# A planned attention kernel: wide QK matmuls dropped where the plan has TensorE columns to spare, and softmax tiles and shifts placed anew

## The chip, the cores and the metric

The kernel runs on one core of one Trainium2 chip. The metric is the device time of one execution in microseconds (us), lower is better. Each number called a median is over several executions; a profile is one further look at one execution, with its span from the first to the last instruction (about 2 us less than the time). All runs quoted here are in the fast state. A ratio is the mean time of one kernel's fast runs over the mean of the other's in the same rounds on the same chip, so it is not quite the ratio of the medians beside it. In the profile PE is TensorE, ACT ScalarE, DVE VectorE, POOL GpSimd, SP the queue that issues most DMAs.

## The reference

```python
B, H, S, Dh = 1, 32, 2048, 20            # all inputs bfloat16
def reference(q, k, v, t):
    eps = 1e-6
    qn = q / (jnp.sqrt((q * q).sum(axis=-1, keepdims=True)) + eps)
    kn = k / (jnp.sqrt((k * k).sum(axis=-1, keepdims=True)) + eps)
    logits = jnp.einsum('bhqd,bhkd->bhqk', qn, kn) * t[None, :, None, None]
    attn = softmax(logits, axis=-1)
    return jnp.einsum('bhqk,bhkd->bhqd', attn, v)
```

There are 32 x 2048 x 2048 exponentials and a head size of only 20, so the exponentials, not the matmuls, are the bulk of the work.

## The kernel before

The work of a head is cut into 16 tiles (128 keys by 2048 queries, four units of 512). Most tiles go through ScalarE, which reads logits in PSUM and writes exponentials. The others go through VectorE, which makes the exponential out of integer arithmetic: one evacuation of PSUM per half tile into int16 (read as fp16), then three shifted copies of the tile. GpSimd takes part of the third shifts. One table says how many tiles of each head VectorE has, another for how many of these GpSimd makes the third shift.

```python
    DVE_TILES = [4, 4, 4, 5, 5, 5, 5, 5, 4, 5, 5, 5, 5, 5, 4, 5, ...]      # sum 153
    KDN = (3, 3, 3, 3, 3, 3, 3, 3, 3, 3, 3, 3, 3, 3, 3, 2, ...)
    # evacuation, two per tile:            DVE
    e.tensor_scalar(xt[sx][:, o:o + W1], psD[:, slot * W1:slot * W1 + W1], X_MUL, X_ADD, ALU.mult, ALU.add)
    # shifts, three per tile of 128 x 2048: DVE, the third one on POOL in pieces of 128 x 512 int32 where KDN says so
    e.tensor_scalar(dst[:, 0:w], x, float(PHASES[i]), None, ALU.add)
```

A QK matmul contracts over 20 values, padded to 32 rows. TensorE runs matmuls of different row groups side by side, so a ScalarE wave of three units (a wave is what one exponential instruction takes) can take one matmul slot (in the trace three such matmuls start within 10 ns, and two of 128 rows 0.22 to 0.23 us apart). Each wave also has a wide form: it feeds 64 or 128 rows, the extra ones zero, which no longer fit beside one another and take one slot more. The wide form computes the same. It exists only to keep TensorE's load up, because a lightly loaded array loses its clock (experiment 3 shows it).

```python
    if len(us) == 3: qk.modes = [("q3", 32, PE_MM + 0.01, 384.0), ("q2", 64, PE_MM * 2, 768.0)]   # rows, us, columns of load
    else:            qk.modes = [("q2", 64, PE_MM, 256.0 * len(us)), ("qk", 128, PE_MM * len(us), 512.0 * len(us))]
```

The whole program is ordered before it runs: a list scheduler with a cost for each task fixes one static order per engine, and the engines then wait for one another by semaphores. The planner repeats this; in each pass it looks at every window of 3.41 us, and where the load of finished matmuls is under 3500 it makes some QK groups wide. It never takes one back.

```python
        heavy = set()
        for _ in range(self.PASSES):
            for t in choice:
                tag, t.rows, t.dur, t.work = t.modes[t in heavy]
            self.list_schedule()
            ...                                   # windows of TICK = 3.41 us, floor LOAD = 3500
                    while i and load < self.LOAD and m >= i:
                        ...
                            more.add(u)
            if not more: break
            heavy |= more
```

## Time and profile before

The median is 667.6 us (666.9 to 668.7, 4 runs).

| | busy us | share | what it does |
|---|---|---|---|
| ACT | 657.1 | 99% | 287 exponentials of 128x1536, 287 of 128x1024, one rest |
| DVE | 654.2 | 98% | 306 evacuations, 365 shifts, small work |
| PE | 601.3 | 90% | QK and PV matmuls; ends are modelled, so this share is too high |
| POOL | 355.3 | 53% | 188 half shifts, norms, scaling |

The page of the kernel before: busy time and clock over the span, the chain that ended last, and the costliest groups (line, engine, operation, output and input, count, busy us, mean ns, idle before).

```profile
span 665.3 us, 14541 instructions
...
PE 601.3 (90%) x5914; PEld 166.3 (25%) x5959; DVE 654.2 (98%) x927; ACT 657.1 (99%) x584; POOL 355.3 (53%) x364
...
PEclk9999999999999999999999999999999999999999
...
ACT 90%; DVE 5%; DMA 1%; SPq 1%; PE 1%; POOL 0%; issue 0%; ACTq 0%
...
L757 ACT ACTIVATE p_ring<-psA 128x1024 bf16<-128x1024 f32 (+1 forms) x575 | 650.0, 1371 | 2.8 <-PE psA L666 2.7
L803 DVE TENSOR_SCALAR xt<-psD 128x1024 int16<-128x1024 f32 x306 | 371.1, 1213 | 4.4 <-PE psD L666 3.3
L821 POOL TENSOR_TENSOR ss<-xt,two 128x512 int32<-128x512 int32 x188 | 236.0, 1256 | 163.2 <-DVE ss L815 83.4
...
L815 DVE TENSOR_SCALAR ss<-xt 128x2048 int16<-128x2048 int16 x365 | 241.8, 683 | 0.9
...
```

ScalarE is busy from its first exponential to its last, and the chain is its exponentials for 89% of the span. VectorE is as full. A reader might stop here and say that nothing can be gained except by moving work. But the records of one engine overlap (the groups' mean of 1371 ns times 575 is 788 us, not 650), so a short wait need not show as idle time. The safer reading is from one start to the next in the timeline: at the median a 128x1536 exponential takes 1.330 us and a 128x1024 one 0.904 us. The sum of what lies above these medians I call the excess. It is 11.0 us for ScalarE, of which the waits view shows 2.7 us:

The waits of ScalarE in the kernel before (who waited for whom: us in total, times, longest).

```profile
...
ACT p_ring L757 <- PE psA L666: 2.7, 4, 1.3
...
```

Of the 11.0 us, 3.8 us are four stalls of over 0.4 us (1.57, 1.20, 0.55 and 0.45 us, behind the exponentials that start at 28.6, 52.6, 209.6 and 221.3 us); the other 7.2 us are small slips. In front of the first three stalls TensorE, whose order is fixed, stood waiting for a DMA or for VectorE (timeline of the kernel before; the wait is in brackets):

```profile
...
30.64 0.37 PE L666 MATMUL psA<-qz,kR 32*128 32x512 bf16 x1 [1.47 <-DMA qz<-qkT]
...
53.93 0.38 PE L666 MATMUL psD<-qz,kR 128*128 128x512 bf16 x1 [0.96 <-DVE xt L803]
...
210.25 0.39 PE L666 MATMUL psD<-qz,kR 64*128 64x512 bf16 x1 [0.73 <-DVE xt L803]
...
```

How much is wide can be counted from the weight loads of QK with 128 rows (groups by shape, kernel before; the count stands after the x):

```profile
...
L666 PEld LDWEIGHTS psA<-qz,kR 128*128 128x128 bf16 x129 | 8.7, 97 | 26.1 <-ACT p_ring L757 24.3 <-issue 1.4
...
L666 PEld LDWEIGHTS psD<-qz,kR 128*128 128x128 bf16 x58 | 4.4, 97 | 7.8 <-DVE xt L803 5.8 <-DVE rec L702 0.5 <-issue 0.5
...
L666 PEld LDWEIGHTS psA<-qz,qkT 128*128 128x128 bf16 x36 | 3.2, 97 | 6.5 <-ACT p_ring L757 5.8 <-issue 0.5
...
L666 PEld LDWEIGHTS psD<-qz,qkT 128*128 128x128 bf16 x20 | 1.8, 96 | 5.2 <-DVE xt L803 3.9 <-issue 1.1
...
```

That is 243 loads. With the three-unit waves of 64 rows it makes the 180 wide groups that the planner reports.

### The profile page before, as it was taken

The numbers are of one execution on the slowest core, as the hardware profiler recorded it, in microseconds if no ns is written. First come the engines' busy times: TensorE is split into PE (matmuls) and PEld (weight loads), VectorE is DVE, ScalarE is ACT, GpSimd is POOL, SyncE is SP. The second block draws the span as 40 slices with busy tenths as digits, with TensorE's granted clock in tenths as the row PEclk, the third lists the DMA queues.
The fourth block names the chain that finished last, engine by engine and source line by source line (L and its number), as shares of the span: only waits on it lengthen the run. The fifth ranks groups of instructions, "written<-read, shape, count | busy, mean of one in ns | idle before, by whom it ended". The sixth has DMA issues, their size and how long they took to land.

```text
span 665.3 us, 14541 instructions
## 1 busy us (share of the span) xinstructions
PE 601.3 (90%) x5914; PEld 166.3 (25%) x5959; DVE 654.2 (98%) x927; ACT 657.1 (99%) x584; POOL 355.3 (53%) x364
## 2 busy tenths in 40 slices
PE   7798989989889999898999999999899989999987
PEld 2222222222222222222222222222222222222221
DVE  8999999999999999999999999999999999999997
ACT  9999999999999999999999999999999999999997
POOL 2346664573655645565365446556466566655622
PEclk9999999999999999999999999999999999999999
DMA  5554434134242442544035142352414415231200
GB/s 64 67 80 76 65 48 78 19 78 54 41 81 21 81 51 45 89 62 75 4 74 62 32 79 28 68 68 44 80 17 91 45 30 81 39 80 11 55 6 11
DMA packets 196723, 36.24 MB, mean 54 GB/s; under 512 B 172592, under 2 KB 196656, under 8 KB 196656
## 3 DMA queue, kind: packets, MB, share of 16 engines
q1 hardware_dynamic: 196512, 35.22, 34.5%
q8 instruction: 47, 0.77, 0.5%
q14 instruction: 20, 0.16, 0.1%
q10 hardware_dynamic: 144, 0.08, 0.1%
HBM read 7.87 MB, written 2.62 MB: 16 GB/s over the span
## 4 chain that ended last, share of the span: by engine, by line
ACT 90%; DVE 5%; DMA 1%; SPq 1%; PE 1%; POOL 0%; issue 0%; ACTq 0%
ACT p_ring L757 89%; DVE xt L803 3%; DVE ss L815 2%; SPq L404 1%; DMA qk_sb<-in_q_dram 1%; DMA qkT<-qkn 0%; ACT qz L450 0%; PE psA L666 0%; PE psD L666 0%; DMA qz<-qkT 0%; POOL qkn L561 0%; POOL ss L821 0%; DVE oT L699 0%; ACT L440 0%; PE psO L686 0%
## 5 line engine op out<-in xcount | busy, mean ns | idle before, releaser
L757 ACT ACTIVATE p_ring<-psA 128x1024 bf16<-128x1024 f32 (+1 forms) x575 | 650.0, 1371 | 2.8 <-PE psA L666 2.7
L803 DVE TENSOR_SCALAR xt<-psD 128x1024 int16<-128x1024 f32 x306 | 371.1, 1213 | 4.4 <-PE psD L666 3.3
L821 POOL TENSOR_TENSOR ss<-xt,two 128x512 int32<-128x512 int32 x188 | 236.0, 1256 | 163.2 <-DVE ss L815 83.4
L666 PE MATMUL psA<-qz,kR 32*128 32x512 bf16 (+2 forms) x1051 | 227.2, 384 | 36.4 <-ACT p_ring L757 27.7
L815 DVE TENSOR_SCALAR ss<-xt 128x2048 int16<-128x2048 int16 x365 | 241.8, 683 | 0.9
L686 PE MATMUL psO<-ss,vph 128*32 128x512 f16 x1836 | 172.9, 385 | 0.1
L686 PE MATMUL psO<-p_ring,vaug 128*32 128x512 bf16 x1436 | 132.9, 384 | 0.1
L666 PE MATMUL psA<-qz,qkT 32*128 32x512 bf16 (+2 forms) x354 | 117.6, 384 | 12.6 <-ACT p_ring L757 10.3
L666 PE MATMUL psD<-qz,kR 64*128 64x512 bf16 (+1 forms) x454 | 120.9, 384 | 7.9 <-DVE xt L803 4.8
L666 PEld LDWEIGHTS psA<-qz,kR 32*128 32x128 bf16 (+2 forms) x1077 | 54.4, 92 | 181.0 <-ACT p_ring L757 176.2
L494 POOL TENSOR_SCALAR vph<-vaug 128x160 f16<-128x160 bf16 (+1 forms) x96 | 40.0, 417 | 80.8 <-DMA vaug<-in_v_dram 39.8
L561 POOL TENSOR_TENSOR qkn<-qk_sb,rs_r 128x640 bf16<-128x640 bf16 x29 | 47.5, 1639 | 37.4 <-DVE ss L815 19.0
L686 PEld LDWEIGHTS psO<-ss,vph 128*32 128x32 f16 x1836 | 44.3, 94 | 81.4 <-issue 56.5
L686 PE MATMUL psO<-xt,vaug 128*32 128x512 f16 x612 | 60.3, 385 | 0.0
L666 PE MATMUL psD<-qz,qkT 64*128 64x512 bf16 (+1 forms) x144 | 54.3, 385 | 1.4 <-DVE xt L803 0.9
L686 PEld LDWEIGHTS psO<-p_ring,vaug 128*32 128x32 bf16 x1436 | 35.7, 94 | 52.4 <-issue 44.1
L666 PEld LDWEIGHTS psD<-qz,kR 64*128 64x128 bf16 (+1 forms) x459 | 29.6, 93 | 68.3 <-DVE xt L803 50.8
L666 PEld LDWEIGHTS psA<-qz,qkT 64*128 64x128 bf16 (+2 forms) x359 | 28.5, 92 | 58.4 <-ACT p_ring L757 55.1
L710 POOL TENSOR_TENSOR o_stage<-oT,rec 128x320 bf16<-128x320 f32 x30 | 29.0, 967 | 18.3 <-DVE ss L815 14.3
L528 DVE TENSOR_REDUCE rs_sum<-sq 128x32 f32<-128x640 bf16 x32 | 25.7, 806 | 0.1
L699 DVE STREAM_TRANSPOSE oT<-psO 128x512 f32<-128x512 f32 x32 | 22.5, 704 | 1.0 <-PE psO L686 1.0
L686 PEld LDWEIGHTS psO<-xt,vaug 128*32 128x32 bf16 x612 | 15.8, 94 | 28.1 <-issue 20.8
(46 smaller groups left out, 87.3 us busy)
## 6 DMA issues: line engine op xcount, KB each, us to landing
kR<-qkT SPq DMA_DIRECT2D x62, 96.0 KB, 2.2
qz<-qkT SPq DMA_DIRECT2D x124, 32.0 KB, 1.8
kR<-qkT SPq DMA_DIRECT2D x62, 64.0 KB, 2.0
qk_sb<-in_k_dram SPq DMA_DIRECT2D x32, 80.0 KB, 2.6
vaug<-in_v_dram SPq DMA_DIRECT2D x32, 80.0 KB, 3.7
qk_sb<-in_q_dram SPq DMA_DIRECT2D x124, 20.0 KB, 2.6
out_dram<-o_stage SPq DMA_DIRECT2D x31, 80.0 KB, 2.2
kR<-qkT SPq DMA_DIRECT2D x62, 32.0 KB, 1.9
```

The source lines that it names most:

```text
L404: return add(eng, name, lambda e, tk: e.dma_start(dst, src), dur, deps, pri, lat=lat, dma=key)
L494: vsc[h] = [add("POOL", f"vs{h}", lambda e, tk, i=i: e.tensor_scalar(vph[bv][:, i, 0:nd, :], vaug[bv][:, R - nd:R, :], 2.0 ** (-PHASES[i] ...
L528: sums.append(dv("sum", lambda e, tk, i=i, sqb=sqb: e.tensor_reduce(rs["sum"][:, 2 * R * i:2 * R * (i + 1)], sqb[:, :, :], AXIS_X, ALU.add ...
L561: u = add("POOL", f"norm{h}", lambda e, tk, x=x, b=b, i=i, j=j: e.tensor_tensor(qkn[b][:, j:j + m, 0:D], x[:, j:j + m, :], bc(rs["r"][:, 2 ...
L666: return eng.matmul(dst, lhsT, mov, tile_position=(p0, 0))
L686: last = eng.matmul(psO[32 * g:32 * g + 32, :], w, rhs_of(g), start=start, stop=False, skip_group_check=True, tile_position=(0, 32 * g))
L699: trO[h] = add("DVE", f"tr{h}", lambda e, tk: e.transpose(oT[:, :, :].rearrange("p r d -> p (r d)"), psO[:, :]), 0.63, [lambda: pv_users[h ...
L710: fin[h] = add("POOL" if pool else "DVE", f"fin{h}", lambda e, tk: e.tensor_tensor(st, src, rb, ALU.mult), TTDUR if pool else 0.40, [rc] + ...
L757: act[w] = add("ACT", f"exp{w}", lambda e, tk: e.activation(p_ring[:, p0 * 512:p0 * 512 + n], psA[:, slot * WAVES[0] * 512:slot * WAVES[0] ...
L803: t1_prev[nchunk[0]] = add("DVE", f"t1.{j}.{k}", lambda e, tk, o=o, slot=slot: e.tensor_scalar(xt[sx][:, o:o + W1], psD[:, slot * W1:slot ...
L815: sh.append([dv(f"s{i}.", lambda e, tk, i=i, dst=dst: e.tensor_scalar(dst[:, 0:w], x, float(PHASES[i]), None, ALU.add), 0.533, war)])
L821: u = add("POOL", f"s{i}.{js[0]}.{c}", lambda e, tk, i=i, dst=dst, c=c, n=n: e.tensor_tensor(dst[:, 2 * c:2 * (c + n)].bitcast(I32), xt[sx ...
```

## The change

The intent: the planner may now also take a wide matmul back where the load of every window that it counts in stays 300 above the floor, so that TensorE has fewer slots to serve and ScalarE and VectorE wait less. Constants of the scheduler and both tables are placed anew for that plan; VectorE gets 154 tiles instead of 153, GpSimd 99 third shifts instead of 94. The diff, cut to its core:

```diff
-    SWITCH = 0.25
+    SWITCH = 0.5
-    PASSES = 10
+    PASSES = 12
+    FIRM = 4
+    MARGIN = 300.0
-    DSL = 0.8
-    HOLDA = 9.0
+    DSL = 0.6
+    HOLDA = 0.7
-    HOLD = {"DVE": 0.0, "PE": HPE}
+    HDV = 0.08
+    HOLD = {"DVE": HDV, "PE": HPE}
...
+            drop, more = set(), set()
+            if k < self.PASSES - self.FIRM:
+                for m, u in enumerate(pe):
+                    if u in heavy and u.modes[1][2] > u.modes[0][2] + 0.02 and \
+                            min(loads[m:hi[m] + 1]) - gain(u) >= self.LOAD + self.MARGIN:
+                        drop.add(u)
...
-            heavy |= more
+            heavy = heavy - drop | more
...
-    SPREAD = 1.0
+    SPREAD = 0.8
-    DVE_TILES = [4, 4, 4, 5, 5, 5, 5, 5, 4, 5, 5, 5, 5, 5, 4, 5, 5, 5, 5, 5, 4, 5, 5, 5, 5, 5, 4, 5, 5, 5, 5, 5]
+    DVE_TILES = [4, 4, 4, 5, 5, 5, 5, 5, 4, 5, 5, 5, 5, 4, 5, 5, 5, 5, 5, 5, 4, 5, 5, 5, 5, 6, 5, 5, 5, 4, 4, 6]
-    KDN = (3, 3, 3, 3, 3, 3, 3, 3, 3, 3, 3, 3, 3, 3, 3, 2, 3, 3, 3, 3, 3, 3, 3, 3, 3, 4, 3, 3, 3, 4, 2, 3)
+    KDN = (4, 5, 2, 4, 3, 2, 4, 4, 2, 2, 4, 3, 3, 3, 4, 2, 4, 3, 3, 4, 3, 3, 5, 2, 3, 5, 2, 4, 2, 3, 3, 2)
+    ACCN = (0, 0, 0, ...)                     # tiles whose third shift a DMA would make: none
...
+        cst = sbuf("cst", [128, 2048], I16)
+        z_cst = memset("POOL", cst[:, :], PHASES[2], 0.3, -70)
```

Left out of this cut are a further step in the choice of what is made wide, a later moment at which GpSimd is asked for its next task, and another choice of which tiles of a head GpSimd helps with. The last two lines belong to a path in which a DMA would add the shift. Its table is all zeros.

## The prediction

> **What bounds the kernel now.** ScalarE and VectorE together. Busy (part 1 of the page): ACT 657.1 us (99%), DVE 654.2 (98%) of 665.3; PE 601.3 (90%, inflated by pipelining), POOL 355.3. The chain of waits is ACT exponentials for 88.8%, unbroken from 222.7 to 660.6 us. Start to start in the timeline, the 128x1536 exponential costs 1.330 us and the 128x1024 one 0.904 (medians); 287 pairs make 641 us, against 652.7 from the first (8.4) to the end of the last (661.1). So ACT loses about 11 us to late matmuls: two stalls of 1.6 and 1.2 us before 55 us, 1 us near 210 to 222, the rest in some 40 slips of 0.05 to 0.3 us that the waits view hides (it shows 2.7 us), because records overlap. DVE is alike: last shift ends 660.6, start-to-start excess about 14 us, half of it dependences of startup and tail. Granted clock 1.00 up to 640 us.
>
> **What the change does.**
> 1. One more head tile goes from ACT to DVE (153 to 154). ACT saves 4/5 of a pair, 1.8 us. DVE gains two evacuations (2 x 1.13 us).
> 2. POOL takes 99 instead of 94 of the third shifts; DVE shifts go from 365 to 363, -1.2 us. DVE net +1.1 us. POOL gains 10 halves of 1.26 us, in windows of DVE's PSUM reads.
> 3. Wide QK matmuls. By weight loads, about 83 two-unit and 58 three-unit ACT groups and 42 DVE groups are wide, some 180; each costs one more matmul slot (about 0.22 us). They only keep TensorE's column load up. The plan may now drop those with over 300 columns to spare; I guess a third to a half go: 13 to 20 us of TensorE time, little of it critical. What counts is the share of ACT's 8 us and DVE's 7 us of slips that such slots caused: I guess a third.
> 4. Ordering constants: small, unknown sign.
>
> The DMA-accumulate path is coded but disabled (all counts zero).
>
> **Clock.** The Trainium skill, "TensorE: Matmul & The Clock Gate" (Part 1: The HAM clock gate), says the array clock halves when a 3413 ns activity window is too idle. The plan's window is the same, its floor of 3500 unchanged; before, that floor gave 1.00, which agrees. But windows now sit nearer the floor.
>
> **Sum.** ACT: -1.8 us work, -2 to -3 us slips. DVE: +1.1 us work, -2 to -4 us slips; it may end later. Startup and the 4 us tail stay. Expected 668.2 - 3.2 = 665.0 us. The gain cannot exceed about 1.8 + 8 us, so over 2% is nearly excluded.
>
> Predicted 665.0 us, range 661.5 to 668.0; faster by over 2%: 0.01, within 2%: 0.97, slower by over 2%: 0.02.
>
> **What would show the steps right.** ACT's pair stays 2.234 us; its start-to-start excess falls from 11 to 7 to 9 us; DVE shifts 363, evacuations 308, POOL shift halves 198; 128-row QK weight loads fall by a third or more, TensorE busy by 10 us or more; clock 0.99 or more.
>
> **What would make it wrong.** Clock under 1 in some stretch, with ACT gaps of microseconds there; POOL's shifts colliding with DVE's two-byte shifts (the Trainium skill, "GPSIMD Engine Reference", 1. Specifications: its SBUF interfaces are shared with VectorE; here shifts stretch from 0.60 to 1.37 us at most), so that DVE ends later; slips that come from ordering, not from wide matmuls.

## The result, and the profile after

The median after is 666.1 us (664.6 to 666.8, 4 runs) against 667.6 before; the ratio is 0.9973, with a 95% interval of 0.9950 to 0.9996. A second set of six runs later gave 666.0 us against 668.0, ratio 0.9966 (0.9952 to 0.9979); expected were 0.996 to 0.999 and the longer spans at the lower clocks, and both came so. So the change gains about 0.3%, some 2 us, far under the 2% from which a verdict would call it faster; but both intervals lie below 1.

The same parts of the page, kernel after:

```profile
span 662.8 us, 14627 instructions
...
PE 579.4 (87%) x5949; PEld 163.2 (25%) x5971; DVE 655.2 (99%) x927; ACT 655.1 (99%) x582; POOL 369.7 (56%) x375
...
PEclk9999999999999999999999999999999999999999
...
ACT 91%; DVE 6%; DMA 1%; issue 1%; PE 0%; SPq 0%; ACTq 0%
...
L785 ACT ACTIVATE p_ring<-psA 128x1024 bf16<-128x1024 f32 (+1 forms) x573 | 647.7, 1402 | 1.5 <-PE psA L694 1.5
L831 DVE TENSOR_SCALAR xt<-psD 128x1024 int16<-128x1024 f32 x308 | 374.9, 1217 | 1.7 <-PE psD L694 0.7
L857 POOL TENSOR_TENSOR ss<-xt,two 128x512 int32<-128x512 int32 x198 | 250.8, 1267 | 171.6 <-DVE ss L851 79.5
...
L851 DVE TENSOR_SCALAR ss<-xt 128x2048 int16<-128x2048 int16 x363 | 243.2, 688 | 0.0
...
```

ScalarE's exponentials fell from 575 to 573 instructions, the evacuations rose from 306 to 308, the shifts of VectorE fell from 365 to 363, GpSimd's halves rose from 188 to 198: just the counts that were foreseen. TensorE's busy time fell by 21.9 us (a rough figure: some matmul records are missing, and two profiles of the kernel after have 579.4 and 586.0 us), and of the wide QK loads only these are left in the groups shown (the planner reports 60 wide groups, before 180):

```profile
...
L694 PEld LDWEIGHTS psA<-qz,kR 128*128 128x128 bf16 x51 | 3.4, 97 | 11.0 <-ACT p_ring L785 10.5 <-issue 0.5
...
L694 PEld LDWEIGHTS psA<-qz,qkT 128*128 128x128 bf16 x15 | 1.4, 97 | 5.0 <-ACT p_ring L785 4.8 <-issue 0.2
...
L694 PEld LDWEIGHTS psD<-qz,kR 128*128 128x128 bf16 x18 | 1.1, 97 | 2.0 <-DVE xt L831 2.0
...
```

Where did the 2.5 us between the two profiled spans come from? ScalarE's time from first to last exponential can be added up: start, plus work at the medians, plus excess. All times in us, from the profiles.

| profile | first exponential starts | work | excess | last one ends | VectorE's last shift ends | span |
|---|---|---|---|---|---|---|
| before | 8.42 | 641.7 | 11.0 | 661.1 | 660.6 | 665.3 |
| after | 9.39 | 640.0 | 9.2 | 658.6 | 657.1 | 662.8 |
| difference | +0.97 | -1.7 | -1.8 | -2.5 | -3.5 | -2.5 |

(Work is the end minus the start minus the excess.) Two terms gain and one loses. The one that loses is at the start. These are the lines of the timeline around it (start us, us, engine, line, operation), first the kernel before:

```profile
...
4.62 0.18 DVE L531 TENSOR_SCALAR rs_u<-rs_sum 128x32 int32<-128x32 int32 x1
...
8.42 1.02 ACT L757 ACTIVATE p_ring<-psA 128x1024 bf16<-128x1024 f32 x1
...
```

and the kernel after:

```profile
...
4.02 1.82 POOL L434 MEMSET cst<- 128x2048 int16 x1
...
4.50 1.38 DVE L559 TENSOR_SCALAR rs_u<-rs_sum 128x32 int32<-128x32 int32 x1
...
9.39 1.02 ACT L785 ACTIVATE p_ring<-psA 128x1024 bf16<-128x1024 f32 x1
```

In the kernel after GpSimd writes the unused constant from 4.02 to 5.84 us. VectorE's first step of the inverse square root, 128x32 integers, took 1.38 us in that time, and 0.18 us before; everything behind it on the way to the first exponential is late. The step ends 35 ns behind the memset. The Trainium skill, "GPSIMD Engine Reference" (8. Key points), says that GpSimd shares its SBUF interfaces with VectorE and contends with it in VectorE's two-port modes or when it has two SBUF inputs. The trace agrees with a collision, though it doesn't show which interface was held. The step has one SBUF input, so by that page it would have to run in a two-port mode; no run here shows its mode.

A last reading of the profile after: VectorE has done its last shift at 657.1 us and then waits 2.0 us for the last matmuls, which wait for ScalarE. The waits of VectorE, kernel after:

```profile
...
DVE oT L727 <- PE psO L714: 2.0, 1, 2.0
...
```

VectorE has more tiles than before and yet ends earlier than ScalarE.

### The profile page after: what moved, and what is told of

The parts are those of the page before. It is cut to its first block, busy times and chain, and to the rows that moved or that the text cites. A ratio compares the mean times of both kernels' runs of the same rounds, so it can differ in the third digit from the quotient of the medians.

```text
span 662.8 us, 14627 instructions
## 1 busy us (share of the span) xinstructions
PE 579.4 (87%) x5949; PEld 163.2 (25%) x5971; DVE 655.2 (99%) x927; ACT 655.1 (99%) x582; POOL 369.7 (56%) x375
## 4 chain that ended last, share of the span: by engine, by line
ACT 91%; DVE 6%; DMA 1%; issue 1%; PE 0%; SPq 0%; ACTq 0%
ACT p_ring L785 91%; DVE xt L831 3%; DVE ss L851 1%; DMA qkT<-qkn 1%; DVE rs_sum L556 0%; DMA qk_sb<-in_k_dram 0%; DVE rs_u L559 0%; DMA qz<-qkT 0%; DVE sq L554 0%; SPq L431 0%; DVE qz L665 0%; DVE oT L727 0%; ACTq L395 0%; DVE kx L673 0%; DVE o_stage L738 0%
## 5 line engine op out<-in xcount | busy, mean ns | idle before, releaser
L831 DVE TENSOR_SCALAR xt<-psD 128x1024 int16<-128x1024 f32 x308 | 374.9, 1217 | 1.7 <-PE psD L694 0.7
L857 POOL TENSOR_TENSOR ss<-xt,two 128x512 int32<-128x512 int32 x198 | 250.8, 1267 | 171.6 <-DVE ss L851 79.5
L694 PE MATMUL psA<-qz,kR 32*128 32x512 bf16 (+2 forms) x1063 | 217.5, 385 | 47.0 <-ACT p_ring L785 42.4
L694 PE MATMUL psA<-qz,qkT 32*128 32x512 bf16 (+2 forms) x354 | 115.4, 384 | 15.0 <-ACT p_ring L785 13.4
L694 PE MATMUL psD<-qz,kR 64*128 64x512 bf16 (+1 forms) x456 | 118.5, 385 | 9.5 <-DVE xt L831 6.5
L694 PEld LDWEIGHTS psA<-qz,kR 32*128 32x128 bf16 (+2 forms) x1074 | 52.9, 92 | 183.1 <-ACT p_ring L785 179.7
L522 POOL TENSOR_SCALAR vph<-vaug 128x160 f16<-128x160 bf16 (+2 forms) x96 | 37.1, 386 | 48.9 <-DVE ss L851 22.5
L694 PE MATMUL psD<-qz,qkT 64*128 64x512 bf16 (+1 forms) x153 | 57.6, 385 | 3.8 <-DVE xt L831 3.3
```

The lines of the kernel that those rows point to most:

```text
L522: vsc[h] = [add("POOL", f"vs{h}", lambda e, tk, i=i: e.tensor_scalar(vph[bv][:, i, 0:nd, :], vaug[bv][:, R - nd:R, :], 2.0 ** (-PHASES[i] ...
L694: return eng.matmul(dst, lhsT, mov, tile_position=(p0, 0))
L831: t1_prev[nchunk[0]] = add("DVE", f"t1.{j}.{k}", lambda e, tk, o=o, slot=slot: e.tensor_scalar(xt[sx][:, o:o + W1], psD[:, slot * W1:slot ...
L857: u = add("POOL", f"s{i}.{js[0]}.{c}", lambda e, tk, i=i, dst=dst, c=c, n=n: e.tensor_tensor(dst[:, 2 * c:2 * (c + n)].bitcast(I32), xt[sx ...
```

## The experiments

My theory after the result: the gain is ScalarE's 1.8 us of moved work; VectorE could take the tile because GpSimd and the new order relieve it; the wide matmuls, by themselves, are worth little, as most stood in TensorE's slack; and the dead memset costs about 1 us. Rivals: each wide matmul costs time wherever it stands; the start is slack; and the granted clock, not the order, makes the difference. All kernels below gave correct results. "Order untouched" means that the plan was made as usual and only then the form of some QK groups was changed, so each engine's order is the same.

### 1. The dead memset taken out (two sets of runs)

```diff
-        z_cst = memset("POOL", cst[:, :], PHASES[2], 0.3, -70)
+        z_cst = None
```

> The kernel after, without the GpSimd memset of a constant tile that nothing reads. Theory (collision at the start): in the profile after, this 1.82 us memset overlaps the first rsqrt step of VectorE, which took 1.38 us there and 0.18 us before, and the first big exponential started at 9.39 us instead of 8.42. Without it the step takes 0.18 us again, the first exponential starts at about 8.4 us, and the time falls by 0.8 to 1.1 us against the kernel after (about 0.9960 of the kernel before, where after is 0.9973). Rival (the start is slack, or the shift of the first wave comes from something else, such as the DMA's landing): the first exponential stays at 9.2 us or later, or it starts earlier and the last one ends where it did.

> The kernel after without the dead memset, a second time, to double the number of runs: first group 0.9968, the kernel after itself 0.9973 and 0.9966. If the 0.95 us by which the first exponential starts earlier reach the end, as the exponentials up to the 160th of that trace say, the ratio is 0.9945 to 0.996 and the spans at full clock are 661.3 to 662.3; if a later wait eats them, 0.9964 to 0.9972.

Measured: 665.1 us against 667.6, ratio 0.9968 (0.9956 to 0.9981); the second time 664.9 us against 667.5, ratio 0.9963 (0.9949 to 0.9977). The orders of the other four engines are identical to those of the kernel after. The timeline of the first of the two:

```profile
...
4.61 0.18 DVE L559 TENSOR_SCALAR rs_u<-rs_sum 128x32 int32<-128x32 int32 x1
...
8.44 1.02 ACT L785 ACTIVATE p_ring<-psA 128x1024 bf16<-128x1024 f32 x1
...
```

The step takes 0.18 us again and the first exponential starts at 8.44 us. In all five profiles of kernels with the memset this step took 1.17 to 1.38 us, and wherever it started (4.50 to 4.72 us) it ended 35 to 37 ns behind the memset; the first exponential started at 9.39 to 9.45. In all nine profiles without the memset the step took 0.18 us and the start was 8.42 to 9.02. So the collision is shown. The start is not slack: the 161st exponential starts at 190.7 us in both profiles, against 191.8 and 192.5 in the two of the kernel after. What reaches the end is less sure. The last exponential ends at 658.1 and 657.9 us, against 658.6 and 660.5. The mean time is 665.0 us over 11 runs against 665.7 over 10 of the kernel after, in different groups of rounds, but the four ratios lie within one another's intervals. The mean spans differ by 0.9 us (662.9 and 663.8). The direction is consistent, the size (0.3 to 1 us) isn't settled: the second ratio falls between the two ranges expected for it. No version seen here is clearly better.

### 2. Wide matmuls made narrow in the order of before

```diff
+        for m, u in enumerate(pe):               # after planning; pe, lo, loads as in the planner
+            hit = [x for x in range(m, len(pe)) if lo[x] <= m]
+            cut = u.modes[1][3] - u.modes[0][3] if u in heavy else 0.0
+            if cut and min(loads[x] for x in hit) - cut >= 3800.0:
+                heavy.discard(u)
+                u.rows, u.work = u.modes[0][1], u.modes[0][3]
+                for x in hit:
+                    loads[x] -= cut
         self.heavy = heavy
```

> The kernel before with its instruction order untouched; of its 180 wide QK groups 134 are made narrow, wherever the plan's column load stays at 3800 or more. Theory A (wide matmuls cost slips): TensorE busy falls by about 20 us, the start-to-start excess of the exponentials falls from 10.9 us by a third or more (to 7 us or less), and of the evacuations from 6.2 us likewise; the time falls by 1 to 3 us, a ratio of 0.996 to 0.9985. Rival B (order and constants gave the smaller slips of the kernel after, and wide matmuls sat in TensorE's slack): TensorE busy falls as much, the excess stays within 1 us, the ratio is 0.999 to 1.001. Rival C (clock): windows nearer to the floor lose the full clock, granted clock under 0.99, and the time rises.

Measured: 667.1 us against 667.6, ratio 1.0004 (0.9990 to 1.0018). TensorE busy fell from 601.3 to 583.1 us, nearly as much as foreseen. The excess of ScalarE was 10.0 us instead of 11.0, the slips in front of the evacuations 7.0 instead of 7.7; two profiles of one kernel differ by 0.7 us (9.7 and 9.0, without the memset) to 2.0 us (9.2 and 11.2, the kernel after) in excess, so 1.0 us is nothing firm; the slips under 0.4 us did not get fewer (7.9 us, before 7.2). Rival B of that expectation holds: 134 wide matmuls of the 180 cost next to nothing where they stood. Two of the five runs had a clock of 0.995 and spans of 666.5, the three others (0.999 and 1.000) 665.0 on average, against 665.4 for the kernel before in the same rounds. So at full clock the narrowing may be worth 0.4 us, and in two runs lost clock more than took it back.

### 3. The same order with none wide at all

```diff
+        for t in choice:
+            t.rows, t.work = t.modes[0][1], t.modes[0][3]
+        heavy = set()
         self.heavy = heavy
```

> The kernel before with its order untouched and no wide QK group at all, so that in 114 places the plan's column load in a window is under its floor of 3500, 2816 at least. If the wide matmuls are needed for the clock, the granted clock falls below 0.99 in some stretch and the time rises by 2 us or more for each window at half clock that hits a busy stretch. If the floor of the plan is over-cautious, the clock stays at 0.995 or more and the time is no worse than with the cut.

Measured: 670.1 us against 667.6, ratio 1.0050 (1.0027 to 1.0073), with clocks of 0.980 to 0.990 in all four runs. The trace shows eight windows of 3.41 us at half clock (lost windows, from here on) before the tail, that is before the last exponential ends; two of them follow one another. The windows view around these two (the stretch in us and its length, the busy us of PE, its weight loads, DVE, ACT and POOL with the number of their instructions, then the clock granted to TensorE, the DMA share and GB/s), with nothing wide:

```profile
...
90.00:98.70 8.70, 6.26 (x60) 1.79 (x56) 8.60 (x11) 8.70 (x10) 5.15 (x5) 1.00 0.57 70
98.70:105.50 6.80, 6.34 (x42) 1.17 (x46) 5.06 (x9) 6.12 (x6) 3.81 (x3) 0.50 0.34 83
105.50:112.30 6.80, 6.80 (x89) 2.10 (x81) 6.43 (x10) 5.82 (x6) 2.14 (x2) 1.00 0.48 77
...
```

and for the same stretches in the kernel before:

```profile
...
90.00:98.70 8.70, 7.39 (x59) 2.05 (x56) 8.66 (x11) 8.70 (x9) 5.25 (x5) 1.00 0.50 70
98.70:105.50 6.80, 6.38 (x75) 1.94 (x77) 6.71 (x12) 6.80 (x7) 4.35 (x4) 1.00 0.34 83
105.50:112.30 6.80, 6.80 (x83) 1.96 (x75) 6.80 (x11) 6.80 (x7) 1.60 (x2) 1.00 0.48 77
...
```

In 6.8 us TensorE finished 42 matmuls instead of 75; VectorE fell to 5.06 of 6.8 us busy, ScalarE to 6.12. The wide matmuls, or at least the 46 that experiment 2 left, are needed. The 2 us for each window that the expectation named were too much: the span is 6.4 us over that of experiment 2, 0.8 us for each of the eight. The Trainium skill, "TensorE: Matmul & The Clock Gate" (Part 1: The HAM clock gate), gives 3413 ns for the window and half rate for a cold array, which this trace agrees with; that zero rows count as load is shown by this pair of kernels only as far as the two differ in nothing else.

### 4. More wide matmuls in the order of after: evenly spread, and in slack

```diff
+        light = [t for t in self.order["PE"] if t.modes and t not in heavy and t.end > self.LIGHT]
+        for x in range(120):
+            u = light[x * len(light) // 120]
+            u.rows, u.work = u.modes[1][1], u.modes[1][3]
+            heavy.add(u)
```

> The kernel after with its order untouched; 120 narrow QK groups, spread evenly, are made wide, 180 in all as before. Theory A (wide matmuls cost slips): the time rises by 2 to 4 us against the kernel after, ratio 1.000 to 1.003 to the kernel before, with exponential excess back at 11 us or more. Rival B (slack): within 0.5 us of the kernel after, ratio 0.9965 to 0.998.

The other run makes 86 wide, each only if TensorE is idle behind it and its consumer later by at least its cost, by the plan; it is built on the kernel without the memset:

```diff
+            cost = u.modes[1][2] - u.modes[0][2]
+            if pe[m + 1].start - u.end >= cost and min(v.start for v in u.users) - u.end - 0.2 >= cost:
+                heavy.add(u)
+                u.rows, u.work = u.modes[1][1], u.modes[1][3]
```

> The kernel after in its own order, without the dead memset, and with 86 more wide QK groups (146 in all), each only where the plan leaves TensorE idle behind it for as long as it costs and its consumer starts that much later anyway. Theory (placement: a wide matmul in slack is free, and it holds the clock): the exponential excess stays within 1 us of the 9.7 us of the kernel without the memset, against 16.9 us when 120 were spread evenly; the runs lose less clock (0.998 or more in most), and the median is 0.2 to 0.8 us under that of the kernel without the memset (665.14), ratio 0.994 to 0.9968. Rival (each wide group costs the same wherever it stands: 120 evenly spread ones cost 6.2 us, 0.05 us each): 86 cost 4.4 us, and the ratio is 1.002 or more.

Measured: 120 evenly spread ones cost 6 us by the medians, 7 by the ratios (672.3 us, ratio 1.0079, 1.0065 to 1.0092), more than either side of the expectation, and brought ScalarE's excess to 16.9 us, at clocks of 0.998 to 1.000. The 86 in slack cost nothing that can be told apart (665.4 us, ratio 0.9963, 0.9952 to 0.9975; excess 10.8 us, 1.1 above the 9.7, with one lost window in the profile), though TensorE was busy for 601.6 us, as much as before the change and more than with the 120 (597.1). So a wide matmul doesn't cost the same wherever it stands, and TensorE's busy time isn't what costs; the place is. The two sets also differ in their number, in their mix (35 and 12 of VectorE's groups) and in the memset, which no run takes apart. This is the same lesson as experiment 2 from the other side. My second hope, that the extra load would win back lost clock, is not shown: the clocks were 0.997 to 1.000, mean 0.998, against 0.997 for the kernel after and 0.997 for that without the memset.

### 5. Rule and tables apart

The kernel before with the new passes of the planner alone (54 wide groups):

```diff
+    PASSES = 12
+    FIRM = 4
+    MARGIN = 300.0
...                                              # the passes as in the change; tables and constants as before
```

> The kernel before with the new dropping rule in its planner and nothing else (tile tables, GpSimd shares and constants of before); planned anew, 54 wide groups instead of 180. With the runs before, this fills the square of rule and tables: neither 1, tables and constants without the rule 1.0003, both 0.9966 to 0.9973. Theory (only the two together pay; with the old tables VectorE's 153 tiles set the end): ratio 0.998 to 1.0015. Rival (the rule pays wherever the plan is made anew): ratio 0.9975 or less, with ScalarE's excess at 9.5 us or less.

The kernel after with the rule out of reach (139 wide groups):

```diff
-    MARGIN = 300.0
+    MARGIN = 1e9
```

> The kernel after with the dropping of wide matmuls switched off (margin out of reach), so that the plan is made anew with 139 wide groups; tables and constants as after. Theory (the drop pays through the order that the plan then finds, not in a given order): the time is 2 to 5 us above the kernel after, ratio 1.000 to 1.004 to the kernel before, with the excess on ScalarE and VectorE as in before or more. Rival (tables and constants carry the gain, the drop nothing): within 0.7 us of the kernel after.

| ratio to before | tables and constants of before | of after |
|---|---|---|
| planner of before, or the rule off | 1 | 1.0003 (0.9990 to 1.0016) |
| dropping rule on | 0.9997 (0.9981 to 1.0014) | 0.9973 and 0.9966 |

Neither half alone gives a gain that can be told from the noise; the two together do. 0.9997 times 1.0003 is 1.0000, against 0.9973 and 0.9966: by the times the halves don't add up, and together they are worth some 2 us more, hardly above the noise of these ratios. The profiles don't settle it. By the end of the last exponential the rule alone takes off 0.6 us (660.5, with a lost window at 32.1 us; the excess is 9.9 us instead of 11.0, or 10.1 at the medians of the kernel before), the tables alone 0.1 us (661.0). Both together take off 2.5 us in the first profile (658.6) and 0.6 us in the second (660.5, with two lost windows). With the tables alone the work falls by 1.7 us, the memset adds 1.0 us at the start (9.45) and the excess is 11.5, with one stall of 1.7 us at 554.3 us in it. With the rule alone VectorE's last shift ends at 660.1 us, almost as late as before, which fits the expectation that its old tables set the end.

Seen from the kernel after, the rule carries the gain: switched off, the time is 2 us longer, as the theory of that run said. Whether that comes from the 79 wide groups more or from the other order that the plan then takes is not separated, and neither are the tables from the constants.

### 6. The tile that moved

The kernel before with one more tile for VectorE, and the kernel after with one less:

```diff
-    DVE_TILES = [..., 5, 5, 5, 5, 5]             # of before, head 31 of 32
+    DVE_TILES = [..., 5, 5, 5, 6, 5]
```

```diff
-    DVE_TILES = [..., 5, 5, 5, 4, 4, 6]          # of after, head 29 of 32
+    DVE_TILES = [..., 5, 5, 4, 4, 4, 6]
```

> The kernel before with one more tile of one head (31st) on VectorE, 154 in all as after, and nothing else. If ScalarE alone bounds the kernel the time falls by 1.8 us (ratio 0.997). If VectorE ends last once it has 154 tiles without any relief (two evacuations and three shifts, 4.1 us more), the exponentials end 2 us earlier, VectorE's last shift 3 to 5 us later, and the time rises by 2 to 5 us (ratio 1.003 to 1.007).

> The kernel after with one tile of the 29th head given back to ScalarE, 153 in all as before; everything else as after, planned anew. Theory (ScalarE's work is the bound in the kernel after): ScalarE has 1.79 us more to do and the time rises by 1.0 to 2.5 us against after, ratio 0.999 to 1.0005, VectorE's last shift well before the last exponential. Rival (VectorE bounds it): the time stays or falls, ratio 0.9975 or less.

Measured: the tile alone costs 4 us (672.0 us, ratio 1.0064, 1.0049 to 1.0078). The end of VectorE's timeline in that run:

```profile
...
662.42 1.23 DVE L803 TENSOR_SCALAR xt<-psD 128x1024 int16<-128x1024 f32 x1
663.68 1.90 DVE L815 TENSOR_SCALAR ss<-xt 128x2048 int16<-128x2048 int16 x3
666.30 0.72 DVE L699 STREAM_TRANSPOSE oT<-psO 128x512 f32<-128x512 f32 x1 [0.72 <-PE psO L686]
...
```

ScalarE's last exponential ended at 659.5 us, 1.6 us earlier than before the change, as its work says; VectorE's last shift ended at 665.6 us. So before the change VectorE was as much the bound as ScalarE, and it could not take a tile.

The tile given back in the kernel after: 666.6 us against 667.5, ratio 0.9989 (0.9973 to 1.0005), 0.0016 to 0.0023 above the kernel after, that is 1.1 to 1.5 us. The end of VectorE's timeline there:

```profile
...
652.55 1.22 DVE L831 TENSOR_SCALAR xt<-psD 128x1024 int16<-128x1024 f32 x1
653.68 2.49 DVE L851 TENSOR_SCALAR ss<-xt 128x2048 int16<-128x2048 int16 x4
661.21 0.72 DVE L727 STREAM_TRANSPOSE oT<-psO 128x512 f32<-128x512 f32 x1 [5.04 <-PE psO L714]
...
```

VectorE is done at 656.2 us and waits 5.0 us; ScalarE's last exponential ends at 660.7. This fits ScalarE alone as the bound of the kernel after, and a moved tile that is worth its 1.79 us of exponentials within the noise; the interval just reaches the rival's 0.9975. What gave VectorE the room is shown only in sum: tables and constants without the rule (experiment 5) end VectorE's last shift at 657.9 us with 154 tiles, 7.7 us earlier than the bare tile does. Of that, five more shifts on GpSimd are 3.0 us (5 x 0.60); the rest should be order, with the placing of the tiles in the last heads and the constants; I did not take it apart.

### 7. A hole filled that was to lose the clock

In a second profile of the kernel after and in that of experiment 4 with the 86 in slack a window at half clock began at 32.1 and 31.9 us, right behind a hole in TensorE's work while the second head's operands were still on their way. Six matmuls of zero weights, accumulated into the open sum, fill the hole:

```diff
+        zero = sbuf("zero", [128, 1], BF16)
+        z_zero = memset("POOL", zero[:, :], 0.0, 0.1, -98)
+        prog.fill = [Task("PE", "fill", lambda e, tk: e.matmul(
+            psO[:, :], bass.AP(zero, 0, [zero[:, :].ap[0], [0, 128]]), ones[:, :], start=False, stop=False,
+            skip_group_check=True), 0.23, [z_one, z_zero], 0.0) for _ in range(6)]
+        ...                                      # after planning: in front of ScalarE's wave 19 in TensorE's order
```

> The kernel after without the dead memset and with six matmuls of zero weights that add zero to the open accumulation, put where TensorE waits 1.5 to 2.4 us for the second head near 28.6 us. In two traces of the kernel after's order a window at half clock began at 31.9 and 32.1 us, just behind this hole. Theory (the hole makes the windows that lose the clock): no half-clock window at 28 to 36 us, mean clock 0.997 or more in nearly all runs, and the mean of the spans 0.3 to 0.8 us under that of the same kernel without the filling. Rival (the lost windows come from elsewhere): clocks and spans as without it. If the filling delays the second head's first matmuls, the first stall near 29 us grows beyond 1.1 to 1.6 us.

Measured: 666.1 us against 667.5, ratio 0.9982 (0.9967 to 0.9997), about 1 us slower than without the filling, and the clocks were no better (0.995 to 1.000, mean 0.9975 against 0.9972). The rival holds: the lost windows come from elsewhere too, at least they didn't go away. The profiled run shows the hole filled and no lost window, but the two profiles without the filling and the memset show none either; so what the hole does isn't settled (the rule alone, experiment 5, also has a lost window at 32.1 us behind such a hole). The profiled run started its first exponential at 8.92 us, half a microsecond late, with 1.0 us of waiting for TensorE's first transposes. Three profiles without filling and memset start as late (8.81 to 9.02), so this need not be the filling; whether the rest of the loss is isn't settled.

### What the clock explains, and what it doesn't

Every run lists its mean granted clock. One window of 3.41 us at half rate takes 0.0026 off the mean of a 664 us span. Mean spans by clock, all fast runs with a clock:

| kernel | 0.999 or 1.000 | 0.997 or 0.998 | 0.996 or less |
|---|---|---|---|
| before | 665.5 (23 runs) | 666.4 (8) | none |
| after | 662.5 (3) | 663.9 (3) | 664.6 (4) |
| after without the memset | 662.8 (5) | 662.8 (3) | 663.0 (3) |

The mean counts the tail too, where no exponential is left to be late: the profile of the tile alone (experiment 6) has 0.997 with its only lost window from 665.5 us on, that of the rule alone 0.997 with one at 32.1 us. So the middle column mixes harmless and harmful windows; 0.996 or less needs one before the tail, as 4.3 us of tail at half rate take only 0.003. No run of 31 of the kernel before stands there, but 4 of 10 of the kernel after: it stands nearer to the floor. With the clock whole (only three runs after) the change gains 3.0 us, over all runs 2.0 us (665.7 to 663.8), so about 1 us of the gain may be lost with the clock. This is a correlation over few runs. In the kernel after one profile shows the mechanism, the windows view of its second profile (span 664.7, clock 0.994):

```profile
...
29.00:32.10 3.10, 1.46 (x21) 0.43 (x19) 2.22 (x4) 2.07 (x3) 1.41 (x1) 1.00 0.29 73
32.10:35.60 3.50, 3.50 (x23) 0.59 (x23) 2.93 (x4) 3.00 (x3) 1.05 (x2) 0.51 0.46 103
35.60:40.00 4.40, 3.79 (x36) 1.03 (x32) 4.36 (x6) 4.40 (x5) 2.31 (x4) 1.00 0.72 84
...
```

and of the first profile (span 662.8, clock 1.000):

```profile
...
32.10:35.60 3.50, 2.91 (x32) 0.81 (x28) 3.50 (x5) 3.50 (x4) 1.04 (x1) 1.00 0.53 115
...
```

In the stretch at 0.51 TensorE did 23 matmuls; in the same stretch of the first profile, at full clock, 32. Beside the two lost windows of the second profile (32.1 and 643.1 us) ScalarE slips by 0.6 us (at 33.2) and by 0.4 and 0.5 us (at 642.8 and 645.4), where the first has no slip of that size. But the third row of the table shows no dependence at all, and neither experiment 4 nor 7 won the clock back. Why some lost windows cost most of a microsecond and others nothing is open; a window's place should matter, and the timed runs have no trace to look it up in.

## Why the prediction was right, point by point

The prediction was 665.0 us, 661.5 to 668.0; the median is 666.1, inside the range. The forecast gain was 3.2 us, the measured one 1.6 us by the first medians and 2.0 us by those of the second set. The hit says little by itself: 667.6 us, no gain at all, lies in the range too. The moved work was foreseen rightly; the gain in slips came out near its size by luck (point 5), and the loss at the start was not in the sum (point 6).

1. **ScalarE and VectorE bound the kernel, and the gain is capped.** Right. One tile more on VectorE without the rest made the kernel 4 us slower (experiment 6), while ScalarE's last exponential ended 1.6 us earlier; ScalarE as the only bound doesn't allow that.
2. **The moved tile saves 1.8 us on ScalarE.** Right: 1.7 us less work in the profile, and 1.1 to 1.5 us in time when it is given back.
3. **VectorE gains 1.1 us of work and may end later.** The work was right (308 evacuations, 363 shifts), the fear wasn't: its last shift ends 3.5 us earlier, at 657.1 us.
4. **A third to a half of the wide matmuls go, 13 to 20 us of TensorE time.** Too small: 120 of 180, and 21.9 us by the profiles. The miss in size mattered little: TensorE's time was not the point (experiments 2 and 4).
5. **Wide matmuls caused a third of the slips.** Wrong as a cause, near in size by luck. ScalarE's excess fell from 11.0 to 9.2 us in the first profile, near the forecast 7 to 9. But the slips under 0.4 us, the 8 us of which the forecast spoke, stayed: 7.2 us before with 180 wide groups, 7.3 after with 60, 7.9 with 46 (experiment 2), 7.4 with none (experiment 3). Only the 120 evenly spread ones raised them, to 15.2. What fell is the long stalls, from 3.8 us (four) to 1.9 us (two), in this one pair of profiles; in front of three of the four TensorE stood waiting for a DMA or for VectorE. Narrowing 134 groups in a given order took nothing measurable off the time; the rule helped only in a plan made anew with the new tables (experiment 5), by a way that is open. The second profile of the kernel after had an excess of 11.2 us, with two half-clock windows in its busy part.
6. **Startup stays.** Wrong, and the clearest miss. A GpSimd memset that nothing reads delayed the first exponential by 0.97 us. The diff showed it, and I took it as harmless because nothing waits for it.
7. **Clock 0.99 or more.** Right as a bound (0.994 to 1.000), but it mattered inside that bound: with the clock whole the gain was 3.0 us (three runs), close to the forecast 3.2 although two of its terms were wrong.

## What to carry to other kernels

Two engines that end within half a microsecond of each other, as here, can be one bound: moving work between them then pays only with relief for the receiver, and each half of such a change, tried alone, can look worthless. Filler work should be judged by where it stands, not only by how much there is: 86 extra wide matmuls in slack were free, 120 spread evenly cost 6 us, and none at all in the old order cost 2.5 us. An instruction that nobody waits for can still delay the critical path, as the memset did; look at what runs beside it. And before a cause is named for many small slips, separate them from the few long stalls: here the one kind changed and the other did not.

## What the Trainium skill lacked or had wrong

- "TensorE: Matmul & The Clock Gate" (Part 1) gives the window (3413 ns, here 3.41) and the half rate (here 0.50), and in its Terms puts the penalty at the throttled time times one half. In this kernel, bound by other engines, eight such windows lengthened the profiled span by 6.4 us against the kernel of experiment 2 in the same order (671.3 to 664.9), 0.8 us a window and not 1.7; that TensorE's slack took the rest is likely but not shown. No page says how much matmul load a window needs.
- "Perfetto Trace Analysis" (Optimizing Scalar/DVE Operations) says, where it gives the fixed data-access overhead of an instruction, that the profiled latency is about twice that, as the write-acknowledgement half overlaps with the next instruction. It doesn't say what follows for reading short waits: of ScalarE's 11.0 us of excess in the kernel before, 2.7 us appear as idle time.
